# Two gelu stores moved to Pool's DMA queue, and the first channel group's normalisation and transposes moved earlier

## The chip, the cores and the metric

The kernel runs on one core of a Trainium2 chip. The core has a matrix engine (PE, with its weight loads shown apart as PEld), a vector engine (DVE), a scalar engine (ACT), a general engine (Pool, POOL in the profile) and a sync engine (SP) that here only issues DMAs. Each engine runs its own instructions strictly in program order and waits on semaphores for the others; DMAs can be issued by SP, ACT or Pool. The metric is the device time of one execution in microseconds (us), as the median of several.

## The reference, cut to what matters

Two blocks stand one behind the other, each with a layer norm, a modulation by vectors made from `c`, and a gated residual. The first is a state-space convolution over a sequence of 2048 tokens with 512 channels. The second is the MLP block around which the change lies:

```python
h = _layernorm(x) * (1 + cb) + sb
# _B_ref(h): x is this h
h = _gelu(_layernorm(x) @ w1)                 # "mix": 512 -> 512
g0..g3 = the four quarters of h's channels, shifted by +1, -1, +2, -2 tokens
x1 = x + concat(g0, g1, g2, g3) @ w2
h2 = _gelu(_layernorm(x1) @ w3) @ w4          # "channel": 512 -> 1376 -> 512
return x1 + h2
```

## The kernel before

The 2048 tokens are held as eight row groups of 256 rows each, `g` = 0 to 7, two tiles of 128 rows each. All products are done in fp32 with both operands split into a high and a low part that the matrix engine takes as float32r: `three` (L835) makes one 128-column piece of a product out of 12 matmuls of 256 columns (high by high and low by high, eight of them, and then high by low, four). So every weight has to be split on the chip before its first use: ACT rounds a piece of it into the high part (`act(h, w)`), DVE subtracts that from the piece and leaves the low part (L756). `split_w(n)` (L1092) does the next n such pieces from a list, in the order in which their loads were issued: four pieces of w3 (columns 0 to 511), four of w4, four of w3 (the next columns), and so on.

Each row group goes through two stages.

- **The w1 stage** ("mix"): `mix_mod1`, `mix_mod2`, `mix_norm` make the normalised rows; `transposed` (L798) transposes them with eight PE transposes into two PSUM tiles `pT0`, `pT1`; `parts_of` (L806) makes the high parts `nh` on ACT and the low parts `nl` on DVE; `mix_half(t, hl, hf)` (L929) does one half of the channels: `mix_w` (L843) has two calls of `three` into a PSUM tile `pm`, ACT takes the gelu of it into an SBUF tile `go`, and `mix_out` (L849) stores `go` to a DRAM scratch `GD`. The pool of `go` has two buffers, so the gelu of one half has to wait until the store of the half two before it has read its buffer.
- **The w2, w3, w4 stage** ("channel"): `chan_load` (L870) reads the four shifted quarters back from `GD` into the tile `win`; `chan_split`, `chan_mod`, `chan_sum` make the product with w2 and the residual; the second layer norm follows (`stats`, `rstd`, then one DVE instruction per tile); then `transposed` and `parts_of` again, and `chan(g, hl)` (L979) does the two large products: `first(f2)` is the w3 product and gelu of 256 of the 1376 columns, `second(f2)` is the w4 product.

The order of all instructions is written out by hand (`tc.manual_schedule()`), and every engine follows it. The change is in the stretch L1245 to L1281, between the last w1 products outside the loop and the first call of `chan`. What stands there, in program order: the w1 product of group 2 (`mix_half(2, ...)` twice, L1245 and L1249) with pieces of group 0's channel stage between; the transposes and parts of group 3 (L1253); the second w2 product of group 0 (`add1 = chan_sum(0, 1)`, L1254); the statistics and the normalisation of group 0 for the w3 product, written out as `stat0(i)` (two DVE instructions and two on Pool, which makes the reciprocal root) and `norm0(i)` (one DVE instruction, L1264), i = 0, 1; the w1 product of group 3 (`mix_half(3, ...)` twice, L1269 and L1274); `transposed(n)` and `parts_of` for group 0 (L1275, L1277); eight calls' worth of `split_w` strewn between; then `chan_add(0)`, `first_stats(4)`, `chan_load(1)`, and the loop over `chan`.

SP issues, in program order, the loads of all pieces of w3 and w4 (`load_w3`, `load_w4`, L1230 to L1244), and behind them the `go` stores of groups 2 and 3 and the reads of `chan_load(1)`. In `chan(0)`, `split_w(4)` follows right behind `first(0)`; `second(0)` needs the first two pieces of w4, and `first(2)` the four pieces of w3's second column group. The row groups 4 to 6 have their w1 stage inside `chan(1)` to `chan(3)`.

Of the kernel before, what the change touches and what calls it, by code (L numbers as in the profile page):

```python
# [102 lines left out]
def dram(t, off, ap):  # L103
    return bass.AP(tensor=t.tensor, offset=t.offset + off, ap=ap)


def body(ctx, tc, A):
    nc = tc.nc
    V, S, P, T, Y = nc.vector, nc.scalar, nc.gpsimd, nc.tensor, nc.sync
# [4 lines left out]
    def act(out, in_, f=AF.Copy, scale=1.0, bias=0.0):  # L114
        return S.activation(out, in_, f, bias=bias, scale=scale)  # L115
# [3 lines left out]
    GD = dpool.tile([4, 128, 20, 128], F32, name="GD")  # L119
# [151 lines left out]
    f2 = lambda t: t.rearrange("p a b -> p (a b)")  # L271
# [187 lines left out]
    def products(k):  # L459
        t, u = divmod(k, 4)  # L460
        tr = trig.pop(k)
        mg = PE[t][0][u]
        e0 = wk.tile([128, 2, 2, 512], F32, name="e0")
        e1 = wk.tile([128, 2, 16, 32], F32, name="e1")
        for a in range(2):
            V.scalar_tensor_tensor(e0[:, 1, a], tr[:, 1, 0], 1.0 - 2.0 * a, mg[:, a], op0=OP.mult, op1=OP.mult)  # L466
        if k == 0:
            weigh(0)
        if u % 2 == 0:
            m1 = m1s[0] = wk1.tile([128, 2, 512], F32, name="m1")  # L470
            pt = PE[t][1][:, u:u + 2].rearrange("p a d c -> p (a d) c")
            V.tensor_mul(m1.rearrange("p a (d x y) -> p (a d) x y", x=4, y=8),
                         pt[:, :, None, :8].to_broadcast([128, 32, 4, 8]),
                         pt[:, :, 8:12, None].to_broadcast([128, 32, 4, 8]))
        V.tensor_mul(e0[:, 0], tr[:, 0, 0:1].to_broadcast([128, 2, 512]), mg)  # L475
        V.tensor_mul(e1.rearrange("p r d q -> p r (d q)"), tr[:, :, 1], m1s[0][:, u % 2:u % 2 + 1].to_broadcast([128, 2, 512]))  # L476
        return e0, e1
# [29 lines left out]
    for k in range(8):  # L507
        w, i = ("w3", k) if k < 4 else ("w4", k - 4)
        n = A[w].shape[0] // 4
# [37 lines left out]
    with tc.manual_schedule():  # L547
# [13 lines left out]
        for k in range(33):  # L561
# [8 lines left out]
            if k < 32:  # L570
# [3 lines left out]
                e = products(k)  # L574
# [89 lines left out]
    def spectrum_k(jh, kc):  # L664
        p = [kbank([128, 2, 2, 128]) for gh in range(2)]
        for i in range(2):
            for ro in range(2):
                for ri in range(2):
                    for kk in range(2):
                        for gh in range(2):  # L670
                            k1 = kc * 4 + 2 * kk + i
                            rows = slice(gh * 64, gh * 64 + 64)
                            w = T2[k1 // 16][rows, k1 % 16]
                            if ri == gh:
                                w = w[:, ro * 64:ro * 64 + 64]
                            elif ro == ri:
                                w = w[:, gh * 64:gh * 64 + 64]
                            else:
                                w = t3s[kc // 2 * 2][rows, k1 % 8]
                            T.matmul(p[gh][kk * 64:kk * 64 + 64, i, ro], w,  # L680
                                     VK[jh][rows, ri * 32 + k1].rearrange("p j g -> p (j g)"),
                                     start=(ri == 0), stop=(ri == 1), skip_group_check=True)
        return p
# [114 lines left out]
    def transposed(x):  # L798
        ps = [psT.tile([128, 2, 256], F32, name=f"pT{j}") for j in range(2)]
        for j in range(2):  # L800
            for i in range(2):
                for k in range(2 * j, 2 * j + 2):
                    T.transpose(ps[j][:, k % 2, i * 128:i * 128 + 128], x[:, i, k * 128:k * 128 + 128], ident)  # L803
        return ps

    def parts_of(ps):  # L806
        hi = [cm.tile([128, 2, 256], F32R, name=f"nh{j}") for j in range(2)]
        lo = [cm.tile([128, 2, 256], F32R, name=f"nl{j}") for j in range(2)]
        for j in range(2):
            act(hi[j], ps[j])  # L810
            V.tensor_sub(lo[j], ps[j], hi[j].bitcast(F32))
        return [hi[k // 2][:, k % 2] for k in range(4)], [lo[k // 2][:, k % 2] for k in range(4)]
# [22 lines left out]
    def three(p, wh, wl, hl, c):  # L835
        hi, lo = hl
        for k in range(4):
            T.matmul(p, wh[:, k, c], hi[k], start=(k == 0), stop=False)  # L838
            T.matmul(p, wl[:, k, c], hi[k], start=False, stop=False)  # L839
        for k in range(4):  # L840
            T.matmul(p, wh[:, k, c], lo[k], start=False, stop=(k == 3))  # L841

    def mix_w(hl, f2):  # L843
        p = psw.tile([128, 2, 256], F32, name="pm")
        for e in range(2):
            three(p[:, e], W1h, W1l, hl, slice((f2 * 2 + e) * 128, (f2 * 2 + e + 1) * 128))
        return p

    def mix_out(g, hf, go):  # L849
        Y.dma_start(dram(GD, (2 + 2 * g) * 128 + hf * 256 * 2560, [[2560, 128], [128 * 2560, 2], [1, 256]]), go)  # L850
        if g not in (0, 7):
            return
        if hf == 0:
            win["pd"] = hv.tile([128, 4, 256], F32R, name="win").bitcast(F32)
        pd = win["pd"][:, hf * 2:hf * 2 + 2]
        gv = go.rearrange("p f (s c) -> p (f s) c", s=2)
        pv = pd.rearrange("p f (s c) -> p (f s) c", s=2)
        if g == 0:
            P.memset(pv[:, :, 127:128], 0.0)
            P.tensor_copy(pv[:, :, 0:96], gv[:, :, 32:128])  # L860
            P.tensor_copy(pv[:, :, 96:127], gv[:, :, 1:32])
        else:
            P.memset(pv[:, :, 0:1], 0.0)
            P.tensor_copy(pv[:, :, 32:128], gv[:, :, 0:96])
            P.tensor_copy(pv[:, :, 1:32], gv[:, :, 96:127])
        Y.dma_start(dram(GD, (18 if g == 0 else 0) * 128 + hf * 256 * 2560, [[2560, 128], [128 * 2560, 2], [1, 256]]), pd)
# [20 lines left out]
    def chan_sum(g, i):  # L887
        wh, wl = win[g]
        p = psm.tile([128, 512], F32, name="ph")
        s = slice(i * 128, i * 128 + 128)  # L890
        for f in range(4):
            T.matmul(p, wh[:, f, s], W2h[:, f], start=(f == 0), stop=False)  # L892
            T.matmul(p, wh[:, f, s], W2l[:, f], start=False, stop=False)  # L893
        for f in range(4):
            T.matmul(p, wl[:, f, s], W2h[:, f], start=False, stop=(f == 3))  # L895
        if i == 1:
            del win[g]
        return lambda: V.tensor_add(cn[g][:, i], cn[g][:, i], p)  # L898
# [24 lines left out]
    def chan_add(g):  # L923
        h = cn.pop(g)
        for i in range(2):
            V.tensor_mul(h[:, i], h[:, i], mods[5])
            V.tensor_add(X2[:, 2 * g + i], X2[:, 2 * g + i], h[:, i])

    def mix_half(t, hl, hf):  # L929
        p = mix_w(hl, hf)  # L930
        go = gop.tile([128, 2, 256], F32, name="go")
        act(go, p, AF.Gelu_apprx_tanh)
        mix_out(t, hf, go)
# [45 lines left out]
    def chan(g, hl):  # L979
# [24 lines left out]
        def half(hf):  # L1004
            if t is not None:
                mix_half(t, st["hl"], hf)
                if t < 6:
                    first_stat(2 * t + 2 + hf)
# [83 lines left out]
    def split_w(n):  # L1092
        for _ in range(n):
            splits.pop(0)()

    steps = [(jh, kc) for jh in range(2) for kc in range(8)]
    with tc.manual_schedule():
# [11 lines left out]
        for n, st in enumerate(steps):  # L1109
            p = spectrum_k(*st)  # L1110
# [85 lines left out]
        hl = parts_of(transposed(mh.pop(7)[0]))  # L1196
        mix_mod2(0, 0)
        mix_mod2(0, 1)
        a10 = inv_half(1, 1, 0, psy, "py")
        a11 = inv_half(1, 1, 1, psy, "py")  # L1200
        mix_half(7, hl, 0)
        mix_norm(0)
        first_stats(1)
        a10()
        mix_half(7, hl, 1)
        mix_mod1(1)
        hl = parts_of(transposed(mh.pop(0)[0]))
# [10 lines left out]
        hl = parts_of(transposed(mh.pop(1)[0]))  # L1218
# [20 lines left out]
        hl = parts_of(transposed(mh.pop(2)[0]))  # L1239
# [12 lines left out]
        add0()  # L1252
        hl = parts_of(transposed(mh.pop(3)[0]))  # L1253
        add1 = chan_sum(0, 1)  # L1254
        split_w(1)
        n = cm.tile([128, 2, 512], F32, name="h2")
        sm = [(cm.tile([128, 2], F32, name="cmv"), cm.tile([128, 1], F32, name="crs")) for i in range(2)]

        def stat0(i):
            stats(sm[i][0], cn[0][:, i])  # L1260
            rstd(sm[i][1], sm[i][0][:, 1:2])

        def norm0(i):
            V.tensor_scalar(n[:, i], cn[0][:, i], sm[i][0][:, 0:1], sm[i][1], op0=OP.subtract, op1=OP.mult)  # L1264

        stat0(0)
        split_w(1)
        add1()
        mix_half(3, hl, 0)  # L1269
        stat0(1)  # L1270
        norm0(0)
        norm0(1)
        split_w(1)
        mix_half(3, hl, 1)  # L1274
        r = transposed(n)  # L1275
        split_w(1)
        r = parts_of(r)  # L1277
        split_w(4)
        chan_add(0)
        first_stats(4)  # L1280
        chan_load(1)  # L1281
        for g in range(8):
            r = chan(g, r)
# [18 lines left out]
```

## Time and profile before

| what | us |
|---|---|
| median of 3 runs | 690.18 |
| lowest and highest of them | 689.29 and 690.67 |
| the profiled execution, its own time | 691.26 |
| its span, from the first to the last instruction | 689.5 |
| PE busy in the span | 642.6 |
| DVE busy | 498.0 |
| ACT busy | 331.2 |
| Pool busy | 124.8 |

The profile is one execution, traced by the hardware. A row of its timeline shows the start, the duration, the engine, the line in the code, the operation with the tile it writes and the one it reads, and, in square brackets, how long the engine stood idle before it and what the profile believes ended that. Durations of neighbours overlap, so the time from one start to the next is what an instruction takes of its engine. Where a wait is for several things at once, the profile names the last event that it saw, which need not be the one that counted. The view by windows gives, for a stretch of time, the busy time of each engine and the TensorE clock that was granted (1.00 is full).

### The profile page before, as it was taken

The numbers are of one execution on the slowest core, as the hardware profiler recorded it, in microseconds if no ns is written. First come the engines' busy times: TensorE is split into PE (matmuls) and PEld (weight loads), VectorE is DVE, ScalarE is ACT, GpSimd is POOL, SyncE is SP. The second block draws the span as 40 slices with busy tenths as digits, with TensorE's granted clock in tenths as the row PEclk, the third lists the DMA queues.
The fourth block names the chain that finished last, engine by engine and source line by source line (L and its number), as shares of the span: only waits on it lengthen the run. The fifth ranks groups of instructions, "written<-read, shape, count | busy, mean of one in ns | idle before, by whom it ended". The sixth has DMA issues, their size and how long they took to land.

```text
span 689.5 us, 16884 instructions
## 1 busy us (share of the span) xinstructions
PE 642.6 (93%) x7195; PEld 509.2 (74%) x7195; DVE 498.0 (72%) x795; ACT 331.2 (48%) x505; POOL 124.8 (18%) x236
## 2 busy tenths in 40 slices
PE   1899999999999998977998999999999999999996
PEld 0456655655569776634887889999899889898895
DVE  7899999999996887986987967464574536363522
ACT  3878988889875557432444623123131312222121
POOL 4011112112103355413741101001010000000000
PEclk9999999999999999998999999999999999999999
DMA  8603264643739997967387010020100201010001
GB/s 299 284 2 79 75 218 105 209 121 85 275 85 317 354 335 258 346 204 226 108 257 240 1 32 32 16 77 15 47 31 17 77 1 62 1 49 13 1 31 31
DMA packets 51091, 86.42 MB, mean 125 GB/s; under 512 B 4676, under 2 KB 39496, under 8 KB 48424
## 3 DMA queue, kind: packets, MB, share of 16 engines
q1 hardware_dynamic: 46712, 66.74, 30.1%
q0 software_dynamic: 3440, 17.57, 7.4%
q8 instruction: 56, 0.92, 0.6%
q10 hardware_dynamic: 864, 1.05, 0.5%
q14 instruction: 19, 0.16, 0.1%
HBM read 59.12 MB, written 32.90 MB: 133 GB/s over the span
## 4 chain that ended last, share of the span: by engine, by line
PE 70%; DVE 6%; DMA 5%; ACT 3%; POOL 2%; issue 1%; ACTq 0%; SPq 0%; DVEq 0%; POOLq 0%
PE pm L841 7%; PE pm L838 7%; PE pm L839 7%; PE xx L448 7%; PE pa L954 6%; PE pa L955 6%; PE pa L962 6%; PE kp L498 3%; DMA ZT<-z 3%; PE ph L893 2%; PE ph L895 2%; PE ph L892 2%; DMA ld<-ZT 2%; PE pu L426 2%; PE pT L803 2%; PE pk L626 2%
## 5 line engine op out<-in xcount | busy, mean ns | idle before, releaser
L115 ACT ACTIVATE gh<-pm 128x512 fp32r<-128x512 f32 (+1 forms) x48 | 26.9, 560 | 200.7 <-PE pm L841 200.7
L838 PE MATMUL pm<-nh,w3h 128*128 128x256 f32 (+1 forms) x352 | 86.6, 281 | 2.7 <-ACT nh L115 2.7
L839 PE MATMUL pm<-nh,w3l 128*128 128x256 f32 (+1 forms) x352 | 86.3, 280 | 0.1
L946 DVE TENSOR_TENSOR gl<-gf,gh 128x512 fp32r<-128x512 f32 (+1 forms) x48 | 30.8, 643 | 68.4 <-ACT gf L115 68.4
L954 PE MATMUL pa<-w4h,gh 128*128 128x512 f32 (+1 forms) x176 | 69.6, 395 | 0.0
L838 PEld LDWEIGHTS pm<-nh,w3h 128*128 128x128 f32 (+1 forms) x352 | 66.0, 187 | 4.4 <-ACT nh L115 2.9
L955 PE MATMUL pa<-w4l,gh 128*128 128x512 f32 (+1 forms) x176 | 68.9, 392 | 0.0
L839 PEld LDWEIGHTS pm<-nh,w3l 128*128 128x128 f32 (+1 forms) x352 | 65.9, 187 | 2.2 <-DVE w3l L756 0.5
L765 POOL TENSOR_TENSOR rs<-mv,eps_t 128x1 f32<-128x1 f32 (+1 forms) x39 | 11.0, 282 | 282.4 <-DVE mv L771 265.4
L841 PE MATMUL pm<-nl,w3h 128*128 128x256 f32 (+1 forms) x352 | 55.0, 278 | 0.0
L449 PE MATMUL xx<-MG,ON 64*128 64x512 f32 x160 | 48.1, 397 | 0.0
L962 PE MATMUL pa<-w4h,gl 128*128 128x512 f32 (+1 forms) x176 | 48.0, 390 | 0.0
L448 PE MATMUL xx<-MG,ON 64*128 64x512 f32 x160 | 48.0, 396 | 0.0
L841 PEld LDWEIGHTS pm<-nl,w3h 128*128 128x128 f32 (+1 forms) x352 | 47.0, 187 | 0.0
L898 DVE TENSOR_TENSOR h<-h,ph 128x512 f32<-128x512 f32 x16 | 11.0, 687 | 45.1 <-PE ph L895 45.1
L466 DVE SCALAR_TENSOR_TENSOR e<-tr,p 128x512 f32<-128x512 f32 x64 | 41.1, 684 | 1.5 <-ACT tr L115 1.5
L498 PEld LDWEIGHTS kp<-e,e 128*32 128x32 f32 x2048 | 30.1, 110 | 12.7 <-issue 7.6
L475 DVE TENSOR_TENSOR e<-tr,p 128x1024 f32<-128x1024 f32 x32 | 39.0, 1220 | 0.0
L476 DVE TENSOR_TENSOR e<-tr,m 128x1024 f32<-128x1024 f32 x32 | 39.0, 1219 | 0.0
L115 ACT ACTIVATE p<-xx 128x1024 f32<-128x1024 f32 (+1 forms) x40 | 37.5, 979 | 2.2 <-PE xx L252 1.0
L962 PEld LDWEIGHTS pa<-w4h,gl 128*128 128x128 f32 (+1 forms) x176 | 33.0, 188 | 7.3 <-DVE gl L946 0.2
L115 ACT ACTIVATE tr<-xx 128x1024 f32<-128x1024 f32 x32 | 33.0, 1030 | 9.6 <-PE xx L449 7.9
(236 smaller groups left out, 1731.6 us busy)
## 6 DMA issues: line engine op xcount, KB each, us to landing
VU<-vs SPq DMA_DIRECT2D x64, 128.0 KB, 3.7
ld<-VU SPq DMA_DIRECT2D x16, 512.0 KB, 7.4
ZT<-z POOLq DMA_DIRECT2D x30, 256.0 KB, 6.2
ld<-ZT SPq DMA_DIRECT2D x12, 512.0 KB
Dw<-in_w POOLq DMA_DIRECT2D x8, 688.0 KB, 4.7
xu<-in_u SPq DMA_DIRECT2D x4, 1024.0 KB, 8.0
KX<-in_x SPq DMA_DIRECT2D x4, 1024.0 KB, 8.0
GD<-go SPq DMA_DIRECT2D x16, 256.0 KB, 2.3
```

Of the source, the lines that this page charges most:

```text
L115: return S.activation(out, in_, f, bias=bias, scale=scale)
L448: T.matmul(x[:, :512], la, ma, start=(i == 0), stop=(i == len(ops) - 1))
L449: T.matmul(x[:, 512:], lb, mb, start=(i == 0), stop=(i == len(ops) - 1))
L466: V.scalar_tensor_tensor(e0[:, 1, a], tr[:, 1, 0], 1.0 - 2.0 * a, mg[:, a], op0=OP.mult, op1=OP.mult)
L475: V.tensor_mul(e0[:, 0], tr[:, 0, 0:1].to_broadcast([128, 2, 512]), mg)
L498: T.matmul(kp[32 * j:32 * j + 32, (k % 2) * 4 + g], e1[:, r, d], e0[:, r, :, d * 32:d * 32 + 32], start=(r == 0), stop=(r == 1), skip_grou ...
L838: T.matmul(p, wh[:, k, c], hi[k], start=(k == 0), stop=False)
L839: T.matmul(p, wl[:, k, c], hi[k], start=False, stop=False)
L841: T.matmul(p, wh[:, k, c], lo[k], start=False, stop=(k == 3))
L954: T.matmul(acc[i], gh[:m, e, s], W4h[:m, f], start=(f == 0), stop=False)
L955: T.matmul(acc[i], gh[:m, e, s], W4l[:m, f], start=False, stop=False)
L962: T.matmul(acc[i], gl[:m, e, s], W4h[:m, f], start=False, stop=(f == 10))
```

## The change

Three things are changed. The `go` stores of row groups 2 and 3 are issued by Pool (`P`) in place of SP (`Y`). The statistics and normalisation of row group 0 stand ahead of most of w3's splits: `split_w` calls of 1, 1, 1, 1 and 4 become 1, 3, 2 and 2 at other places. And the transposes and parts of row group 0 are issued in the middle of the last w1 product outside the loop, between its two calls of `three`, by a function `between` that is handed down. Every product, split and store is still done, with the same shapes.

```diff
-    def mix_w(hl, f2):
+    def mix_w(hl, f2, between=None):
         p = psw.tile([128, 2, 256], F32, name="pm")
         for e in range(2):
             three(p[:, e], W1h, W1l, hl, slice((f2 * 2 + e) * 128, (f2 * 2 + e + 1) * 128))
+            if e == 0 and between:
+                between()
         return p
 
     def mix_out(g, hf, go):
-        Y.dma_start(dram(GD, (2 + 2 * g) * 128 + hf * 256 * 2560, [[2560, 128], [128 * 2560, 2], [1, 256]]), go)
+        q = P if g in (2, 3) else Y
+        q.dma_start(dram(GD, (2 + 2 * g) * 128 + hf * 256 * 2560, [[2560, 128], [128 * 2560, 2], [1, 256]]), go)
...
-    def mix_half(t, hl, hf):
-        p = mix_w(hl, hf)
+    def mix_half(t, hl, hf, between=None):
+        p = mix_w(hl, hf, between)
...
         add1 = chan_sum(0, 1)
-        split_w(1)
...
         stat0(0)
-        split_w(1)
         add1()
-        mix_half(3, hl, 0)
         stat0(1)
         norm0(0)
+        split_w(1)
         norm0(1)
-        split_w(1)
-        mix_half(3, hl, 1)
-        r = transposed(n)
-        split_w(1)
-        r = parts_of(r)
-        split_w(4)
+        split_w(3)
+        mix_half(3, hl, 0)
+        split_w(2)
+
+        def turn0():
+            nh.append(parts_of(transposed(n)))
+
+        nh = []
+        mix_half(3, hl, 1, turn0)
+        r = nh[0]
+        split_w(2)
         chan_add(0)
         first_stats(4)
         chan_load(1)
```

## The prediction, made before the changed kernel was run

> **What bounds the kernel now.** The page's busy times came first, then the view by windows over the second half of the run, to see from where on nothing but PE counts.
>
> ```profile
> PE 642.6 (93%) x7195; PEld 509.2 (74%) x7195; DVE 498.0 (72%) x795; ACT 331.2 (48%) x505; POOL 124.8 (18%) x236
> ...
> 371.70:374.40 2.70, 0.03 (x1) 0.03 (x1) 1.23 (x2) 2.69 (x6) 0.00 (x0) 0.90 0.34 118
> 374.40:377.30 2.90, 2.90 (x13) 2.90 (x14) 2.90 (x6) 2.48 (x5) 0.00 (x0) 0.50 0.91 248
> ...
> 386.00:420.00 34.00, 34.00 (x215) 30.48 (x215) 25.22 (x43) 11.02 (x23) 0.89 (x2) 1.00 0.10 32
> 420.00:500.00 80.00, 80.00 (x520) 72.47 (x519) 45.17 (x80) 21.62 (x39) 10.46 (x28) 1.00 0.11 34
> ```
>
> A row of windows has the stretch, its length, then busy time and count of PE, PEld, DVE, ACT and POOL, then the granted clock, the DMA share and GB/s. From 386 on PE is busy all the time (34.00 of 34.00, 80.00 of 80.00): whatever reaches 386 earlier ends earlier by as much. Just before, there is a hole of 2.7 us without a matmul, and behind it 2.9 us in which PE had only 0.50 of its clock. The change edits this stretch. So I read PE's timeline there.
>
> ```profile
> 364.95 0.28 PE L838 MATMUL pm<-nh,w1h 128*128 128x256 f32 x1
> ...
> 367.79 0.28 PE L838 MATMUL pm<-nh,w1h 128*128 128x256 f32 x1
> ...
> 370.65 1.04 PE L803 MATMUL pT<-ident,h 128*128 128x128 f32 x8
> 374.37 0.58 PE L838 MATMUL pm<-nh,w3h 128*128 128x256 f32 x1 [2.69 <-ACT nh L115]
> ...
> 378.56 0.28 PE L838 MATMUL pm<-nh,w3h 128*128 128x256 f32 x1
> ...
> 384.08 0.28 PE L838 MATMUL pm<-nh,w3h 128*128 128x256 f32 x1
> ...
> 386.17 0.28 PE L838 MATMUL pm<-nh,w3h 128*128 128x256 f32 x1
> ```
>
> These are the starts of `mix_half(3)`'s two halves, of the transposes of `n`, of `first(0)`, `first(1)`, `first(2)` and of `first(2)`'s second `three`. A half of 24 matmuls takes 370.65 - 367.79 = 2.86, one `three` 1.43. PE loses: 2.69 in the hole; 378.56 - 374.37 - 2.86 = 1.33 in `first(0)` at half clock; 386.17 - 384.08 - 1.43 = 0.66 in `first(2)`. Together **4.7 us**, the ceiling of what this stretch can give. The hole ends with `nh` on ACT, so ACT and SP come next.
>
> ```profile
> 355.91 0.60 ACT L115 ACTIVATE go<-pm 128x512 f32<-128x512 f32 x1 [3.52 <-PE pm L841]
> ...
> 359.19 0.58 ACT L115 ACTIVATE go<-pm 128x512 f32<-128x512 f32 x1
> ...
> 362.90 1.15 ACT L115 ACTIVATE w3h<-w3l 128x512 fp32r<-128x512 f32 x2
> 371.71 0.60 ACT L115 ACTIVATE go<-pm 128x512 f32<-128x512 f32 x1 [7.66 <-PE pT L803]
> ...
> 373.72 1.08 ACT L115 ACTIVATE nh<-pT 128x512 fp32r<-128x512 f32 x2
> 374.67 2.20 ACT L115 ACTIVATE w4h<-w4l 128x512 fp32r<-128x512 f32 x4
> ```
>
> ```profile
> 363.81 1.71 SPq L750 DMA_DIRECT2D w4l<-Dw  x3
> 365.93 7.77 SPq L850 DMA_DIRECT2D GD<-go  x4
> 373.80 1.85 SPq L873 DMA_DIRECT2D win<-GD  x4
> ```
>
> ```profile
> 370.00:371.60 1.60, 1.60 (x15) 1.44 (x14) 0.00 (x0) 0.00 (x0) 0.00 (x0) 1.00 0.22 76
> 371.60:372.30 0.70, 0.08 (x1) 0.00 (x0) 0.00 (x0) 0.59 (x2) 0.00 (x0) 1.00 0.02 7
> ```
>
> ACT stands idle for 7.66 us before the gelu of group 3's first half, though that product was complete by about 367.95 (the next half starts at 367.79). The row names `pT`, which the gelu doesn't read; what it does need is its `go` buffer, last used by group 2's first gelu, done at 356.51. That buffer's store stands in SP's queue behind the weight loads and is issued at 365.93, 9.4 us after its data was ready; DMA traffic dies away at 371.6 (76 GB/s before, 7 after), and ACT goes on at 371.71. I take the store's landing, about 5.7 us after issue, as the true releaser. The `w3h` splits, both gelus and then `nh` queue behind it on ACT.
>
> DVE has its own part in it:
>
> ```profile
> 365.76 0.68 DVE L898 TENSOR_TENSOR h<-h,ph 128x512 f32<-128x512 f32 x1
> 366.47 0.70 DVE L770 BATCH_NORM_STATS2 st<-h 128x6 f32<-128x512 f32 x1
> 367.20 0.18 DVE L771 BATCH_NORM_AGGREGATE cmv<-st 128x2 f32<-128x6 f32 x1
> 367.30 0.52 DVE L1264 TENSOR_SCALAR h<-h,cmv,crs 128x512 f32<-128x512 f32 x1
> 368.53 0.55 DVE L1264 TENSOR_SCALAR h<-h,cmv,crs 128x512 f32<-128x512 f32 x1 [0.71 <-POOL crs L766]
> ...
> 374.47 1.28 DVE L811 TENSOR_TENSOR nl<-pT,nh 128x512 fp32r<-128x512 f32 x2
> 375.67 2.49 DVE L756 TENSOR_TENSOR w4l<-w4l,w4h 128x512 fp32r<-128x512 f32 x4
> 378.07 0.69 DVE L926 TENSOR_TENSOR h<-h,modg 128x512 f32<-128x512 f32 x1
> ...
> 382.35 0.66 DVE L946 TENSOR_TENSOR gl<-gf,gh 128x512 fp32r<-128x512 f32 x1
> 382.93 2.49 DVE L756 TENSOR_TENSOR w3l<-w3l,w3h 128x512 fp32r<-128x512 f32 x4
> ```
>
> From 374.47 DVE has no pause until the four `w3l` of `first(2)`, which end at 385.4, just where PE stalls. So DVE, not PE, decides how much of the 4.7 us comes back.
>
> **The change, part by part.** *Stores on Pool.*
>
> ```profile
> 356.58 0.19 POOL L828 TENSOR_TENSOR nm<-nm,rs 128x1 f32<-128x1 f32 x1
> 365.34 0.54 POOL L765 TENSOR_TENSOR crs<-cmv,eps_t 128x1 f32<-128x1 f32 x1 [8.57 <-DVE cmv L771]
> ```
>
> ```profile
> L706 POOL DMA_DIRECT2D ZT<-z x30: 528/550/632, 233.5 to 300.1; - x30
> ...
> DMA to landing us min/median/max: 2.9/6.2/8.9
> ```
>
> ```profile
> q0 software_dynamic: 660, 2.93, 49.2%
> ...
> PA<-in_PA POOLq DMA_DIRECT2D x1, 256.0 KB, 4.7
> C<-in_C POOLq DMA_DIRECT2D x1, 256.0 KB, 15.6
> ```
>
> Pool is idle from 356.77 to 365.34, so it issues the first store at about 356.8 and the second at 359.8, for 0.55 us each, off every path. The reciprocal roots that stand behind them on Pool are wanted at 364.7 at the earliest. No `go` store was seen on Pool's queue. Bounds from other 256 KB transfers there: 2.9 us (fastest `ZT` store) to 15.6 (`C`, last of five at the start, behind 2.7 MB). I take 6.2, the median of 30 `ZT` stores of the same size, issued beside SP's loads as here: landed at 363.0 and 366.0. The gelus want the buffers at 367.95 and about 371.7, so even 8.9 is early enough. For group 3 the stores follow the gelus; `chan_load(1)` reads rows up to group 2 alone, and on SP it no longer waits behind a gelu: it goes out right after the loads, at about 366 in place of 373.80. `chan_load(2)`, which reads group 3, stands behind `second(4)` of the loop's first pass, over 20 us later.
>
> A rule speaks against this edit: the Trainium skill, "DMA: Bandwidth & Descriptors", section "Issuing engines are not separate DMA queues", says that DMAs of all issuers interleave on the same 16 engines, so that another issuer saves only the time to initiate, usually small. By that rule the store is no faster once issued, which I don't assume either; what SP's rows show is that the time to initiate is 9.4 us here, not small. The rival "no earlier" below is that rule taken at its word.
>
> *Normalisation ahead of the splits.* Without the two splits on DVE, `add1` waits only for the w2 product (next PE work starts at 364.95): about 365.15 in place of 365.76, 0.6 earlier. The chain behind it keeps its steps: the second `norm0` follows the start of its aggregate by 368.53 - 367.20 = 1.33, so at 367.9, done by 368.5.
>
> *Transposes inside the product.* They come after the third `three`, at 364.95 + 3 x 1.43 = 369.2. `n` is ready at 368.5: no wait, 0.7 to spare. They take 0.9 on PE wherever they stand; the last `three` follows to about 371.7. Under it ACT and DVE make the parts: ACT does the first gelu at 368.0 (0.5), two `w4h` (2.20 / 4 = 0.55 each) to 369.6, `nh` at 369.9 and 370.4. DVE does `norm0` until 368.45, then five splits at 0.6 (2.49 for four), to 371.45, then the two `nl` (0.6 each) to 372.65. `first(0)` can start at 371.7 without a hole; its first eight matmuls need `nh` alone (0.95), so `nl` is wanted at 372.65 and 372.9: just in time. So the hole and the half clock behind it go: 374.37 becomes 371.7.
>
> *What is late next.* DVE, after `nl`: two more `w4l`, for which ACT is ready at 372.9 and 373.4 (second gelu at 371.75, then `w4h`), so to 374.15 with a 0.3 pause; `chan_add` starts there in place of 378.07. That is **3.9 us earlier**, and everything behind on DVE keeps its order, so the `w3l` of `first(2)` come 3.9 earlier as well, at 381.5. PE alone would come 4.2 earlier to them and waits 0.3 more. **The sum is 3.9 us.** In the profiled execution 691.26 becomes 687.4 (span 685.6). That execution lies 1.08 above the median shown; for the median, 690.18 - 3.9 = **686.3 us**. That the half clock may not be there in every execution does not change it, since DVE sets the 3.9.
>
> On that clock: the Trainium skill, "TensorE: Matmul & The Clock Gate", section "Why this matters for your kernels", asks for idle gaps over about 3 us before the clock drops. Here 2.69 us were enough (granted 0.50), so the measurement decides. By the rule the ceiling would be 1.3 lower, and 3.4 us an end for the sum.
>
> **The rivals.**
>
> - *PE alone decides* (chance 0.07): if DVE's pauses are shorter than I took, all 4.7 us come back: 685.5. For it: `gl` at 382.35 is close to PE's need already. Against it: DVE's unbroken row of work.
> - *No earlier* (0.08): Pool's store shares the DMA engines with SP's loads and lands near 371.6 after all. Then ACT's first gelu stays at 371.7, two `w4h` and `nh` behind it, `nl` about 374.0 and, with two `w4l` in place of four behind it, `chan_add` at 376.5: 1.5 gained, 688.7. For it: the 15.6 row (from 356.8: 372.4). Against it: that one stood last in its queue, and here nothing is ahead.
> - *Slower* (0.05): Pool's queue is the one that the profile calls software; a `go` store has, by the code, 256 runs of 1 KB against 64 of 4 KB for `ZT`, and if the time went by runs: 4 x 6.2 = 25, landing at 381.6. It decides from 373.1 on, where the 1.5 above is used up: 8.5 slower, 698.7. Against it: `PA`, 128 runs, landed in 4.7, no more than `ZT` with 64.
> - *No change* (0.04): one of the tight steps (`n` 0.7 early, `nl` just in time, the window for `chan_split(1)`) makes a wait as long as the old one: 690.
>
> **How the numbers follow.** The forecast has 0.76, with a range of its own from 685.5 to 687.3: 4.7 to 2.9, the latter if DVE has another pause of 1 us. For 8 in 10 with the spread of the runs before (0.9 below the median): 685.2 to 688.7, which takes in the rival "no earlier". A measurement here tells about 0.2%, 1.4 us, from no change: faster 0.89 (forecast, PE alone, most of "no earlier"), same 0.06, slower 0.05.
>
> **What would show it.** Right: the store on Pool issued near 357, ACT's gelu of group 3 near 368 with a short wait, transposes between two `three` of `mix_half(3)`, no hole before `first(0)`, granted clock 1.00 from 365 to 380, `chan_add` about 374, a stall of up to 1 us left in `first(2)`. Wrong: ACT still idle until after 370 before that gelu, PE waiting for `n` at the transposes or for `nl`, or ACT waiting for the window.

## The result, and the profile after

Timed in turns with the kernel before, the changed kernel took 684.39 us (median of 6, 682.67 to 685.1) against 689.39 (median of 6): a ratio of 0.9927 with a 95% interval of 0.9908 to 0.9946. A second and longer timing, 12 runs against 35, gave 685.12 against 689.21, ratio 0.9937 (0.9917 to 0.9957), which is 4.1 us less. So it is faster, by 5.0 us in the first timing and 4.1 in the second, where 3.9 were forecast; and the first time lies 0.8 us below the low end of the range, 685.2.

The profiled execution of the changed kernel took 684.35 us, span 682.6. That is 6.9 us less span than in the first profile of before, and not all of it belongs to the change. PE's timeline of both kernels is the same up to the transposes of row group 3 and again from the first w4 product of `second(1)` on; between them lies all that the change edits. I call that **the stretch** and use its length as the measure. In the first profile of before it runs from 361.29 to 387.59. Here are its ends in a second profile of the unchanged kernel before, and then in the changed kernel:

```profile
359.59 1.04 PE L803 MATMUL pT<-ident,h 128*128 128x128 f32 x8
...
385.69 0.39 PE L954 MATMUL pa<-w4h,gh 128*128 128x512 f32 x1
```

```profile
358.64 1.04 PE L803 MATMUL pT<-ident,h 128*128 128x128 f32 x8
...
366.57 1.04 PE L803 MATMUL pT<-ident,h 128*128 128x128 f32 x8
368.87 0.28 PE L838 MATMUL pm<-nh,w3h 128*128 128x256 f32 x1
369.82 1.10 PE L841 MATMUL pm<-nl,w3h 128*128 128x256 f32 x4
370.76 0.28 PE L838 MATMUL pm<-nh,w3h 128*128 128x256 f32 x1
...
371.70 0.62 PE L841 MATMUL pm<-nl,w3h 128*128 128x256 f32 x4
...
377.61 0.28 PE L838 MATMUL pm<-nh,w3h 128*128 128x256 f32 x1
...
379.57 0.28 PE L838 MATMUL pm<-nh,w3h 128*128 128x256 f32 x1
...
380.93 0.39 PE L957 MATMUL pa<-w4h,gh 128*128 128x512 f32 x1
```

The stretch is 26.30 and 26.10 us before, 22.29 after: **4.0 and 3.8 us shorter**. Ahead of it the two profiles of before differ by 1.7 us (361.29 and 359.59) with nothing changed; that is what drifts from one execution to the next. Behind it, from the first w4 product of `second(1)` to PE's last matmul, both profiles of both kernels take 296.3 us. One small gain lies outside the stretch: from PE's last matmul to the end of the span it takes 5.34 to 5.39 us in the eight profiles of kernels with stores on Pool, and 5.57 to 5.61 in the six others. So about 0.2 us of the timed gain is at the end of the program; nothing was run to find out why. In the changed kernel the hole is gone: `first(0)` starts at 368.87, behind a product that ends there. Two losses are left on PE. The first `three` of `first(0)` takes 370.76 - 368.87 = 1.89 in place of 1.43, and the first one of `first(2)` 379.57 - 377.61 = 1.96: 0.46 and 0.53 us.

ACT's, Pool's and SP's timelines, and the DMA view of 350 to 380 (the last number is the median time from issue to landing):

```profile
356.52 0.58 ACT L115 ACTIVATE go<-pm 128x512 f32<-128x512 f32 x1
...
365.39 0.60 ACT L115 ACTIVATE go<-pm 128x512 f32<-128x512 f32 x1 [2.95 <-issue]
365.88 1.14 ACT L115 ACTIVATE w4h<-w4l 128x512 fp32r<-128x512 f32 x2
367.20 1.09 ACT L115 ACTIVATE nh<-pT 128x512 fp32r<-128x512 f32 x2 [0.18 <-PE pT L803]
369.11 0.60 ACT L115 ACTIVATE go<-pm 128x512 f32<-128x512 f32 x1 [0.82 <-ACT nh L115]
```

```profile
354.41 0.80 POOL L853 DMA_DIRECT2D GD<-go  x1 [0.28 <-issue]
357.39 0.73 POOL L853 DMA_DIRECT2D GD<-go  x1 [2.18 <-ACT go L115]
...
364.69 0.89 POOL L766 TENSOR_TENSOR crs<-crs,pw 128x1 f32<-128x1 f32 x1
```

```profile
364.89 2.73 SPq L876 DMA_DIRECT2D win<-GD  x4
```

```profile
GD<-go POOLq DMA_DIRECT2D x4, 256.0 KB, 5.6
```

The stores leave 0.3 to 0.6 us after their gelu, where group 2's first one took 9.4. They are four, two halves of each of two groups; the title's two are those of group 2, whose buffers group 3's gelus need. Group 3's first gelu starts 365.39 - 358.64 = 6.75 us into the stretch; before it was 371.71 - 361.29 = 10.42. `nh` follows at 367.20, while PE is still at the last w1 product.

The windows show the clock (the number ahead of the last two), and DVE's timeline shows what paces the rest:

```profile
362.00:369.00 7.00, 7.00 (x60) 6.92 (x60) 6.00 (x12) 3.16 (x6) 2.78 (x5) 1.00 1.07 358
369.00:372.30 3.30, 3.21 (x27) 2.95 (x26) 3.27 (x7) 1.64 (x3) 0.73 (x1) 1.00 0.57 202
372.30:380.00 7.70, 7.61 (x53) 6.80 (x52) 7.60 (x15) 6.12 (x11) 2.13 (x4) 1.00 0.01 2
```

```profile
363.95 0.18 DVE L771 BATCH_NORM_AGGREGATE cmv<-st 128x2 f32<-128x6 f32 x1
...
365.61 0.55 DVE L1266 TENSOR_SCALAR h<-h,cmv,crs 128x512 f32<-128x512 f32 x1 [0.45 <-POOL crs L766]
366.07 1.89 DVE L756 TENSOR_TENSOR w3l<-w3l,w3h 128x512 fp32r<-128x512 f32 x3
367.88 1.28 DVE L756 TENSOR_TENSOR w4l<-w4l,w4h 128x512 fp32r<-128x512 f32 x2
369.08 1.28 DVE L811 TENSOR_TENSOR nl<-pT,nh 128x512 fp32r<-128x512 f32 x2
370.28 1.28 DVE L756 TENSOR_TENSOR w4l<-w4l,w4h 128x512 fp32r<-128x512 f32 x2
371.49 0.68 DVE L929 TENSOR_TENSOR h<-h,modg 128x512 f32<-128x512 f32 x1
...
376.33 2.49 DVE L756 TENSOR_TENSOR w3l<-w3l,w3h 128x512 fp32r<-128x512 f32 x4
```

PE has its full clock throughout. DVE has no pause from 365.61 until the stretch ends; `nl` is done at 370.36, and PE's four `nl` matmuls that begin at 369.82 take nearly twice as long as their like at 371.70 (1.10 against 0.62): that is the 0.46, read to a few hundredths.

### The profile page after: what moved, and what is told of

The parts are those of the page before. It is cut to its first block, busy times and chain, and to the rows that moved or that the text cites. A ratio compares the mean times of both kernels' runs of the same rounds, so it can differ in the third digit from the quotient of the medians.

```text
span 682.6 us, 16886 instructions
## 1 busy us (share of the span) xinstructions
PE 639.0 (94%) x7195; PEld 506.5 (74%) x7195; DVE 498.1 (73%) x795; ACT 331.4 (49%) x505; POOL 128.2 (19%) x240
## 4 chain that ended last, share of the span: by engine, by line
PE 73%; DVE 5%; DMA 4%; ACT 3%; POOL 2%; issue 1%; ACTq 0%; SPq 0%; DVEq 0%; POOLq 0%
PE xx L448 7%; PE pm L841 7%; PE pm L839 7%; PE pm L838 7%; PE pa L957 6%; PE pa L958 6%; PE pa L965 6%; PE kp L498 4%; PE pk L680 3%; DMA w4l<-Dw 2%; PE pk L626 2%; PE pu L426 2%; PE pz L702 2%; PE ph L896 2%; PE ph L898 2%; PE ph L895 2%
## 5 line engine op out<-in xcount | busy, mean ns | idle before, releaser
L448 PE MATMUL xx<-MG,ON 64*128 64x512 f32 x160 | 47.1, 390 | 0.0
L449 PE MATMUL xx<-MG,ON 64*128 64x512 f32 x160 | 47.1, 390 | 0.0
```

What stands on the lines that cost most here:

```text
L448: T.matmul(x[:, :512], la, ma, start=(i == 0), stop=(i == len(ops) - 1))
L449: T.matmul(x[:, 512:], lb, mb, start=(i == 0), stop=(i == len(ops) - 1))
```

## The experiments

All times of the stretch are read as above, from one profile each; two profiles of the same kernel gave 26.30 and 26.10, and 22.29 and 22.35, so a difference of 0.2 us or less between two kernels is not told apart. Gains in the stretch are against 26.2. The ratios are of timed runs against the kernel before, with their 95% intervals.

| kernel | stretch, us | gained | ratio |
|---|---|---|---|
| before, again | 26.10 | | 0.9998 (0.9976 to 1.0021) |
| changed, again | 22.35 | 3.9 | 0.9937 (0.9917 to 0.9957) |
| stores on Pool alone | 24.47 | 1.7 | 0.9973 (0.9952 to 0.9994) |
| new order alone | 25.64 | 0.6 | 0.9979 (0.9955 to 1.0002) |
| changed, transposes behind the product | 22.57 | 3.6 | 0.9938 (0.9918 to 0.9957) |
| changed, two splits ahead of the normalisation | 22.27 | 3.9 | 0.9947 (0.9926 to 0.9968) |
| changed, group 3's gelus into other buffers, stores on SP | 22.37 | 3.8 | 0.9930 (0.9904 to 0.9956) |
| changed, stores on ACT | 22.80 | 3.4 | 0.9938 (0.9916 to 0.9961) |
| before, hole filled with matmuls | 26.12 | 0.1 | 0.9994 (0.9977 to 1.0010) |
| changed, `nl` ahead of `w4l` | 22.27 | 3.9 | 0.9933 (0.9910 to 0.9956) |
| changed, `first_stats(4)` later | 21.69 | 4.5 | 0.9931 (0.9908 to 0.9953) |
| the last two together | 21.25 | 4.9 | 0.9920 (0.9901 to 0.9939) |

The timed intervals are 1.1 to 1.8 us wide to each side, so they tell the kernels with the change's whole gain from before (and the stores alone, just), but not the new order alone, and not these kernels from one another; that is read from the stretch.

**Both kernels again.** No edit.

> The kernel before, unchanged, for a second profile and more times. The stretch is measured from the start of the transposes of row group 3 (pT, 361.29 in the first profile) to the first w4 product of second(1) (pa, 387.59): 26.30 us. Theory (the change acts in this stretch alone, and what the two first profiles differ by ahead of it, 2.65 us, is drift between executions): the stretch is 26.3 within 0.4 again, while the start of the stretch moves by 1 us or more from 361.29. Rival (the changed kernel is faster ahead of the stretch as well, by a lasting effect): the stretch starts within 0.5 of 361.29 again, and at 358.6 in every profile with the changed order.

> The changed kernel, unchanged. Theory: the stretch is 22.3 within 0.3 as in its first profile (22.29), so 4.0 shorter than before; the timed difference to the kernel before, in many alternating rounds, is 4.0 us (ratio 0.9942), and the 5.0 of the first timing was 1 us of scatter. Rival: the difference is 5.0 us or more again (ratio 0.9927 or less), so something outside the stretch gains 1 us.

The stretch was 26.10 and 22.35, its start 359.59 and 358.78. In the other profiles with the changed order it started anywhere from 357.86 (other buffers) to 361.16 (stores on ACT). So the rival, a lasting gain ahead of the stretch, falls; the 2.65 us there were drift. The timed difference is 4.1 us, near the theory's 4.0; its interval, 3.0 to 5.7, does not exclude 5.0 by itself, but the profiles show no place for a fifth microsecond: 3.8 to 4.0 in the stretch and 0.2 at the end.

The second profile of the kernel before also names what ACT waits for in another way than the first, where the row had `pT`:

```profile
369.85 0.60 ACT L115 ACTIVATE go<-pm 128x512 f32<-128x512 f32 x1 [7.50 <-DMA GD<-go]
```

Here it is the store itself.

**The stores alone.** The diff's lines in `mix_out`, in the kernel before.

```diff
-        Y.dma_start(dram(GD, ...
+        q = P if g in (2, 3) else Y
+        q.dma_start(dram(GD, ...
```

> The kernel before with the go stores of groups 2 and 3 issued by Pool, the order otherwise as before. Theory (ACT waits for the store of group 2's first half): group 3's first gelu starts within 0.3 us of the end of its product, the hole on PE shrinks from 2.69 to about 0.9, the clock stays at 1.00 behind it, chan_add starts 1.9 us earlier relative to the start of the stretch: stretch 24.4, 1.9 us gained. Rival (the gelu waits for the transposes that the profile names, not for the store): ACT stays idle until the transposes, nothing gained.

```profile
359.02 1.04 PE L803 MATMUL pT<-ident,h 128*128 128x128 f32 x8
```

```profile
365.77 0.60 ACT L115 ACTIVATE go<-pm 128x512 f32<-128x512 f32 x1 [3.99 <-PE pm L841]
```

The stretch was 24.47 against 24.4 expected, and the gelu came 365.77 - 359.02 = 6.75 us into it. So ACT did wait for the store, and the name for the releaser in the first profile of before was the wrong one. One thing was not expected. Pool's timeline and a row of DVE:

```profile
366.67 0.75 POOL L851 DMA_DIRECT2D GD<-go  x1 [2.41 <-ACT go L115]
367.43 0.20 POOL L765 TENSOR_TENSOR crs<-cmv,eps_t 128x1 f32<-128x1 f32 x1
367.71 0.57 POOL L766 TENSOR_TENSOR crs<-crs,pw 128x1 f32<-128x1 f32 x1
```

```profile
368.32 0.55 DVE L1265 TENSOR_SCALAR h<-h,cmv,crs 128x512 f32<-128x512 f32 x1 [2.77 <-POOL crs L766]
```

In the old order the second `stat0` stands behind `mix_half(3, hl, 0)`. So its two instructions on Pool stood behind a store that waited 2.41 us for its gelu, and DVE waited 2.77 us for them. Here it cost little: PE waited 0.16 us for that part of `n`, and ACT, with a gelu and a split in between, began `nh` only at 369.64. In the changed order the reciprocal root stands ahead of that store.

**The order alone.** The changed kernel with `q = Y`.

> The changed order of normalisation, splits and transposes, with all go stores on SP as before. Theory: ACT still waits for the store until about 371.7 on the clock of the first profile, 10.4 us into the stretch; PE waits for nh about 1.6 us; chan_add 1.5 earlier relative to the stretch: stretch 24.8, 1.5 us gained. Rival (the reordering alone is what gains, the queue does not matter): stretch 22.3, 4.0 us gained.

ACT, PE, a window with the granted clock, and DVE:

```profile
371.18 0.60 ACT L115 ACTIVATE go<-pm 128x512 f32<-128x512 f32 x1 [6.62 <-PE pm L841]
```

```profile
373.35 0.39 PE L838 MATMUL pm<-nh,w3h 128*128 128x256 f32 x1 [2.20 <-ACT nh L115]
```

```profile
374.90:378.30 3.40, 3.40 (x17) 3.40 (x18) 3.33 (x6) 0.67 (x2) 0.00 (x0) 0.54 0.84 230
```

```profile
376.04 0.68 DVE L929 TENSOR_TENSOR h<-h,modg 128x512 f32<-128x512 f32 x1
```

ACT waits as before, and `chan_add` comes 376.04 - 360.76 = 15.28 us into the stretch, 1.5 earlier than the 16.78 of before: that is what was expected. But the stretch is 25.64 and not 24.8. PE stood idle for 2.20 us, its clock then was about half for 3.4 us, and with DVE now ahead of it PE set the end: it has no wait from 373.35 to the end of the stretch at 386.40. Stores and order gain 1.7 and 0.6 alone and 3.9 together; each one alone leaves a wait that the other one takes away.

**The buffer, without Pool.** The changed order, all stores on SP, but group 3's gelus write to the buffers of `gf`, which are not yet in use.

```diff
-        q = P if g in (2, 3) else Y
+        q = Y
...
-        go = gop.tile([128, 2, 256], F32, name="go")
+        go = c2p.tile([128, 2, 256], F32, name="gf") if t == 3 else gop.tile([128, 2, 256], F32, name="go")
```

> The changed order with all go stores on SP as before, but the gelus of group 3 write into two buffers of another pool (the one of gf, not yet in use), so that they need no store of group 2 to have landed. Theory (what ACT waits for is the buffer, freed by the store): group 3's first gelu starts at the end of its product, about 6.75 us into the stretch, as with Pool's stores, and the stretch is 22.3 within 0.3. Rival (Pool's queue helps in another way, by the earlier read of the window or by relieving SP): the gelu or another step is late, stretch 24 or longer.

```profile
364.61 0.60 ACT L115 ACTIVATE gf<-pm 128x512 f32<-128x512 f32 x1 [2.96 <-PE pm L841]
```

The gelu starts 364.61 - 357.86 = 6.75 us into the stretch and the stretch is 22.37. With the same order and the stores on SP the gelu came at 10.42 when it wrote to `go` (the order alone). So it was the buffer; Pool's queue is one way to free it early.

**The stores on ACT.** `q = S if g in (2, 3) else Y` in the changed kernel.

> The changed kernel with the go stores of groups 2 and 3 issued by ACT, right behind each gelu, in place of Pool. Theory (any queue that is not behind the weight loads does): ACT pays about 0.4 for each issue, nh comes 0.2 later, nl not at all: stretch 22.3 to 22.6. Rival (it takes Pool's own queue): the store lands as late as SP's, stretch 25.6 as with the order alone.

```profile
368.49 0.37 ACTq L853 DMA_DIRECT2D GD<-go  x1
368.90 1.15 ACT L115 ACTIVATE w4h<-w4l 128x512 fp32r<-128x512 f32 x2 [0.44 <-DMA w3l<-Dw]
```

The stretch was 22.80: the queue does as well as Pool's, but each issue holds ACT up by about 0.4 us. The next split starts 0.44 late, and DVE paused 0.41 for a `w4h` of which nothing was expected. So the range of 22.3 to 22.6 was missed by 0.2. Pool's queue is nothing special; Pool has the time to issue.

**The transposes behind the product.** In the changed kernel `mix_half(3, hl, 1)` and then `turn0()`.

> The changed kernel with the transposes and parts of row group 0 behind the last w1 product again, not inside it; stores on Pool and the new order of splits stay. The stretch (group 3's transposes to the first w4 product of second(1)) was 26.30 and 26.10 in two profiles of before and 22.29 and 22.35 in two of the changed kernel. Theory (DVE paces): PE waits 0.4 for nh, nl and chan_add come 0.2 later: stretch 22.5, 0.2 lost. Rival (the transposes inside the product are what hides the wait for nh): first(0) 1 us later or more, stretch 23.3 or longer.

```profile
371.01 0.39 PE L838 MATMUL pm<-nh,w3h 128*128 128x256 f32 x1 [0.35 <-ACT nh L115]
```

22.57, and a wait of 0.35: the transposes inside the product are worth 0.2 to 0.3 us, little more than two profiles of one kernel can differ by.

**Two splits ahead of the normalisation.** One `split_w(1)` behind `add1 = chan_sum(0, 1)` and one behind `stat0(0)` again, then `split_w(2)` behind `norm0(1)`.

> The changed kernel with two of w3's splits ahead of the normalisation again, at their old places before and behind stat0(0). Theory: n is done 0.8 later, 0.1 before PE reaches its transposes, and DVE fills a pause with a split: no wait, stretch 22.3 within 0.2. Rival (the normalisation had to come first): PE waits for n at the transposes by 0.5 or more and the stretch is 22.8 or longer.

22.27: no wait, as expected. That the normalisation stands ahead of these two splits gains nothing here.

**What paces the end.** First the kernel before with matmuls in its hole:

```diff
+        wu = psm.tile([128, 512], F32, name="pa0", bufs=1)
+        for _ in range(10):
+            T.matmul(wu, W1h[:, 0, :128], W1h[:, 0], start=True, stop=True)
         r = parts_of(r)
```

> The kernel before with ten more matmuls of 512 columns (2.2 us, into a PSUM bank not yet in use, their result unused) between the transposes of row group 0 and first(0), in the hole. Theory (DVE paces the end of the stretch, so the half clock behind the hole is hidden): granted clock 1.00 behind the hole, first(0) 1.3 shorter, but gl and first(2) wait for DVE by as much: stretch 26.0 to 26.3, nothing gained. Rival (the half clock costs what it takes): stretch 24.9, 1.3 gained.

A window, and PE's next wait:

```profile
374.00:377.30 3.30, 3.30 (x28) 3.12 (x28) 3.30 (x6) 2.42 (x6) 0.00 (x0) 1.00 0.71 196
```

```profile
382.41 1.21 PE L962 MATMUL pa<-w4h,gl 128*128 128x512 f32 x4 [0.68 <-DVE gl L946]
```

The clock is full, `first(0)` is quicker, and PE then waits 0.68 for `gl` where it had not waited before; the stretch is 26.12. In before, DVE hid the half clock, to within the 0.2 us that can be told.

Then three edits to the changed kernel: `first_stats(4)` from behind `chan_add(0)` to behind the `split_w(4)` that follows `first(3)`; on DVE the two `nl` ahead of the two `w4l` (ACT keeps its order); and both.

> The changed kernel with first_stats(4), 1.6 us of DVE that nothing needs for 20 us, taken from between chan_add(0) and first(0) and put behind the splits that follow first(3). Theory (DVE paces the end of the stretch): gl and the w3l pieces of first(2) come 1.6 earlier, the stall of 0.53 in first(2) goes, stretch 21.8, 0.5 gained beyond the change. Rival (PE or ACT paces): stretch stays 22.3.

> The changed kernel with the two nl pieces ahead of the two w4l pieces on DVE, first_stats(4) at its place. Theory (DVE paces): the wait of 0.46 in first(0) goes, but chan_add and all behind it on DVE stay where they are, and PE waits longer in first(2): stretch 22.2 to 22.3. Rival (PE paces): stretch 21.8.

> As the run with first_stats(4) moved, and on DVE the two nl pieces stand ahead of the two w4l pieces that were in front of them (ACT's order unchanged). Theory: PE's wait of 0.46 for nl in first(0) goes as well, and with first_stats(4) out of the way DVE has room for it: stretch 21.3, 1.0 gained beyond the change. Rival (nl was not what first(0) waited for, or the wait moves to first(2)): 21.8 as with first_stats(4) moved alone.

With `first_stats(4)` later, the ends of the stretch:

```profile
358.41 1.04 PE L803 MATMUL pT<-ident,h 128*128 128x128 f32 x8
...
380.10 0.39 PE L957 MATMUL pa<-w4h,gh 128*128 128x512 f32 x1
```

The first `nl` matmuls of `first(0)` with `nl` first:

```profile
370.59 0.63 PE L843 MATMUL pm<-nl,w3h 128*128 128x256 f32 x4
```

With `first_stats(4)` later: 21.69, 0.6 gained. With `nl` first: 22.27, nothing gained, though PE's wait in `first(0)` had gone (0.63 in place of 1.10). With both: 21.25, 1.1 gained. So `nl` is worth 0.4, but only where DVE has the room; DVE paces the end of the stretch in the changed kernel too. The last is the fastest version that was run: 684.20 us against 689.37. By the stretch it is 1.1 us ahead of the changed kernel; the timed runs can't tell the two apart.

## Why the prediction was right, and where it was not

- **What bounds the kernel** held: the stretch is where the time went, and everything behind it moved by as much, and by 0.2 us more at the very end, which the prediction did not have.
- **The releaser.** Against the row of the first profile, the prediction took the store's landing for what ACT waited for; the second profile of before names that store. Two kernels that take that wait away by different means, a store on another queue and another buffer, both bring the gelu to 6.75 us into the stretch (forecast: 368.0 - 361.29 = 6.7).
- **The store on Pool.** An issue took 0.73 to 0.80 and not 0.55; the landing median was 5.6 against the 6.2 that was taken. Neither mattered. With 256 runs its median was no later than that of `ZT` with 64, so the rival by runs falls.
- **Normalisation.** `n` was ready at 366.16, 0.4 us before PE's transposes at 366.57 and not 0.7: the second `norm0` followed its aggregate by 365.61 - 363.95 = 1.66 and not 1.33, as Pool's last step for it took 0.89 us and not the 0.55 of before. With two splits ahead of it `n` was in time as well, so this part of the change gained nothing of its own; the prediction gave it no price.
- **Transposes.** "Just in time" for `nl` was 0.46 us too hopeful: `nl` is done at 370.36, and PE wanted the first of it at 369.82. It cost nothing, since DVE paced the end.
- **DVE sets the sum.** `chan_add` was forecast at 374.15 on the first profile's clock, 12.86 into the stretch; it came at 371.49 - 358.64 = 12.85. So close an agreement is partly luck: `nl` ended 11.72 us into the stretch where the sum has 11.36, and the pause of 0.3 that the sum has behind `nl` took that up. The stretch lost 4.0 and 3.8 us in place of 3.9. PE's losses left over are 0.46 and 0.53, together 0.99: about the stall of up to 1 us that was forecast, but in two places. The filled hole and the later `first_stats(4)` show the reason to be right. The filled hole also answers the 3.4 us that the prediction gives as an end for a hole without a half clock: the stretch stayed 26.12 with a full clock, so about 3.8 would still have been there to gain.
- **Where it failed: the base.** The step that failed is "for the median, 690.18 - 3.9 = 686.3". It took the median of three runs for the kernel's time, and the low end, 685.2, left 1.1 below that sum. The kernel before had a median of 689.39 in the six runs timed beside the changed kernel and of 689.21 in 35 later ones, so the base was 0.8 to 1.0 too high. With 689.21 the same 3.9 gives 685.3, and the changed kernel measured 685.12 in 12 runs. The first measured 684.39 lies 0.7 under that: the same kernel timed twice, so I take it for scatter between timings, and what makes it stays open. The profile had a warning in it that I put aside: 691.26 for the profiled execution, 1.08 above that median, where the three lay within 1.4 of one another; later runs of before went from 687.1 to 695.59.
- **A price that was wrong:** the rival "no earlier" was to gain 1.5. The new order with SP's late stores is that case, and it gained 0.6. `chan_add` did come 1.5 earlier; what was left out, by the trace, is the half clock behind the remaining hole; no run takes it away in that kernel. "That the half clock may not be there in every execution does not change it" holds only while DVE is behind PE.

## What to carry to other kernels

Look for what a waiting instruction really needs, buffers to be freed by a store among it: here a store behind some fifteen loads on one queue was late by the loads' time, and Pool's queue, ACT's queue and a spare buffer each took that away. Before an instruction is moved to an idle engine's queue, look at what then stands behind it there, for it waits as well. And price a change from the stretch between two points that the edit leaves alone, with a base of many runs; a median of three was off by as much as a quarter of the gain here.

## What the runs showed of the hardware

Behind an idle gap of 2.20 us on PE the granted clock was 0.54 over 3.4 us (new order alone); behind gaps of 0.35 us (transposes behind the product), 0.49 us (stores alone) and 1.64 us (at 299.45 in the run with the filled hole) it stayed full. With the hole of before filled it stayed at 1.00 too, so the idle time is what brings it down there. The Trainium skill, "TensorE: Matmul & The Clock Gate", section "Why this matters for your kernels", names gaps over about 3 us; here less sufficed, as in the two profiles of before, with 2.69 and 2.52 us. A store of 256 runs of 1 KB from Pool's queue held Pool for 0.73 to 0.80 us, one of 64 runs of 4 KB for 0.55 in the median (runs counted from the code). The same store issued from ACT took 0.37 us at its queue, and a gap of 0.44 us stood before the engine's next instruction both times that it was in front of a split (one row names a load, the other the gelu ahead; I take the issue for the cause).
